# Delta rule and MLP: chunks of 32 tokens with all batches in a step, and the small inverses on VectorE

## The chip, the cores and the metric

The kernel runs on one NeuronCore of a Trainium2 chip. The metric is the device time of one execution, in microseconds (us). The core has a matrix engine (TensorE, PE in the profile; PEld is its loading of the stationary operand), three engines for elementwise work (VectorE = DVE, ScalarE = ACT, GpSimd = POOL) and SyncE (SP), which here only issues DMAs. TensorE writes to PSUM, 8 banks of 2 KB on each of 128 partitions; all else lies in SBUF.

## The reference

An attention block by the delta rule feeds an MLP. There are 4 batches, 8 heads, 768 tokens and a head dimension of 48; the MLP has 3072 tokens, 384 features and 2048 hidden units. All is float32.

```python
k_n = k / (np.linalg.norm(k, axis=-1, keepdims=True) + 1e-06)
for t in range(S):
    y[:, :, t] = einsum('bhd,bhde->bhe', q[:, :, t], state)
    v_old = einsum('bhde,bhd->bhe', state, k_n[:, :, t])
    state = state + beta_t * einsum('bhd,bhe->bhde', k_n[:, :, t], v_t - v_old)
x = y.transpose(0, 2, 1, 3).reshape(B * S, H * D)
h = x @ w_in
out = (h * clip(h + 3, 0, 6) / 6) @ w_out
```

## The kernel before

The tokens of a batch are cut into 6 chunks of C = 128; a step is one chunk of one batch with all 8 heads, so there are 24 steps, ordered so that batches 0 and 1 take turns and then batches 2 and 3. In a chunk that starts with the state S0, with L[i, j] = beta_j k_i.k_j for j < i, the kernel solves (I + L) Z = V - K S0, gives Y = Q S0 + strict_lower(Q K^T diag(beta)) Z, and adds (diag(beta) K)^T Z to the state.

For each step, `prep` (L260 to L273) normalises the keys and multiplies them by beta on GpSimd. `inverse` (L300 to L389) transposes k, q and beta k on TensorE, forms the scores in PSUM (L322, on 64 rows of the array per head), masks them, and inverts the four 32 x 32 diagonal blocks of I + L by doubling the size of inverted blocks: four levels, each with two sets of 8 matmuls (L362 and L370) of 128 x 128 stationary and 32 moving columns, between which GpSimd and VectorE spread a compact matrix into a full one (`to_full`, L283). `MX` (L385) couples the blocks. `chain` (L395 to L477) is the serial part: R = V - K S0 (L416), three rounds of U (L406), Z (L406), Y (L442, L447), the state's update (L457, L467), and the transposes of Y into `xT` (L474). `mlp_block` (L480 to L513) takes 256 tokens: 16 hidden slices of 3 matmuls (L486), each followed by a ScalarE and a VectorE instruction (L491, L495), then 2 x 16 matmuls into the output (L503).

The loop at the end takes one piece of `chain(i)`, one of `inverse(i + 1)` and one of the MLP in turn. The tile framework treats the order in which the program emits instructions as a priority; the order of each engine's queue is fixed when the program is built, and on a queue an instruction waits for the semaphores of what it needs. The weights arrive as float64 bits; `load_rows` (L167 to L199) makes float32 of them in seven VectorE instructions a piece, eight pieces a step. All loads of q, k, v and the stores of the output are issued on SP's queue, those of the weights on GpSimd's.

Of the kernel before, what the change touches and what calls it, by code (L numbers as in the profile page):

```python
# [8 lines left out]
FP32 = mybir.dt.float32  # L9
# [8 lines left out]
def kernel(  # L18
# [23 lines left out]
    C, G, DP = 128, 32, 64  # L42
    NG = C // G
    NLEV = 5
    assert 2**NLEV == G and S % C == 0 and D <= DP and H % 4 == 0 and B % 2 == 0
    NCH = S // C
    NP = H // 2
    BH = B * H
    NKT = DM // 128
    NFC = FF // 128  # L50
    assert NKT * 128 == DM == H * D and NFC * 128 == FF and BH <= 128
    CB = 2
    TB = CB * C
    assert NCH % CB == 0
# [7 lines left out]
    psT = ctx.enter_context(tc.tile_pool(name="psT", bufs=1, space=PSUM))  # L62
    psA = ctx.enter_context(tc.tile_pool(name="psA", bufs=1, space=PSUM))
    psL = ctx.enter_context(tc.tile_pool(name="psL", bufs=2, space=PSUM))
    psC = ctx.enter_context(tc.tile_pool(name="psC", bufs=1, space=PSUM))
    psM = ctx.enter_context(tc.tile_pool(name="psM", bufs=2, space=PSUM))

    steps = [(g * 2 + i, c) for g in range(B // 2) for c in range(NCH) for i in range(2)]
    N = len(steps)
    kfs, vfs, invs, Fs = {}, {}, {}, {}  # L70

    def tokens(ap, i):
        b, c = steps[i]
        return ap[b, :, c * C : (c + 1) * C, :].rearrange("h t d -> t h d")

# [1 line left out]
    NKB, NBKB = 2, 3  # L77
    kbufs = [persist.tile([C, NP, 2, DP], FP32, name=f"kb{i}") for i in range(NKB)]
    qbufs = [persist.tile([C, NP, 2, DP], FP32, name=f"qb{i}") for i in range(NKB)]
    bkbufs = [persist.tile([C, NP, 2, DP], FP32, name=f"bkb{i}") for i in range(NBKB)]  # L80

    def heads(t):
        return t[:].rearrange("p a e w -> p (a e) w")[:, :, 0:D]

    def load_k(i):
        if i < N:
            kfs[i] = stage.tile([C, H, D], FP32, name="kf")
            nc.sync.dma_start(out=kfs[i][:], in_=tokens(k, i))

    def load_v(i):  # L90
        if i < N:
            vfs[i] = stage.tile([C, H, D], FP32, name="vf")
            nc.sync.dma_start(out=vfs[i][:], in_=tokens(v, i))

    def load_q(i):
        if i < N:
            nc.sync.dma_start(out=heads(qbufs[i % NKB]), in_=tokens(q, i))

    load_k(0)
    load_k(1)  # L100
    beta_fm = persist.tile([BH, S], FP32, name="beta_fm")
    nc.scalar.dma_start(out=beta_fm[:], in_=beta.rearrange("b h s -> (b h) s"))

    for t in kbufs + qbufs + bkbufs:
        nc.vector.memset(t[:, :, :, D:DP], 0.0)
    load_q(0)
    load_q(1)
    load_v(0)
    load_v(1)
    load_k(2)  # L110
    load_k(3)

# [4 lines left out]
    def select(view, pattern, base, mult, op=ALU.is_ge):  # L117
        nc.gpsimd.affine_select(
            out=view, in_=view, pattern=pattern, compare_op=op, fill=0.0, base=base,
            channel_multiplier=mult,  # L120
        )

    masks = []
    for lev in range(NLEV):
        # The lower left block of each 2s x 2s diagonal block, transposed.
        s = 2**lev
        m = const.tile([C, C], FP32, name=f"mask{lev}")
        mv = m[:].rearrange("p (b e s) -> p b e s", e=2, s=s)
        nc.gpsimd.memset(m[:], 0.0)
        nc.gpsimd.memset(mv[:, :, 1, :], 1.0)  # L130
        nb = C // (2 * s)
        select(m[:], [[-2 * s, nb], [0, 2 * s]], 0, 1)
        select(m[:], [[2 * s, nb], [0, 2 * s]], s - 1, -1)
        masks.append(m)
    mrest = const.tile([C, C], FP32, name="mrest")
    nc.gpsimd.memset(mrest[:], 1.0)
    select(mrest[:], [[G, NG], [0, G]], -1, -1)
    mdiag = const.tile([C, NG, G], FP32, name="mdiag")
    nc.gpsimd.memset(mdiag[:], 1.0)
    select(mdiag[:], [[-G, NG], [0, G]], 0, 1)  # L140
    select(mdiag[:], [[G, NG], [0, G]], G - 1, -1)
    mstrict = const.tile([C, C], FP32, name="mstrict")
    nc.gpsimd.memset(mstrict[:], 1.0)
    select(mstrict[:], [[1, C]], 0, -1, ALU.is_gt)

# [21 lines left out]
    def load_rows(dst, src, w):  # L167
        """Float32 rows of a weight matrix. It may come as the bits of float64: sign, 11 bits of
        exponent, 52 of mantissa, low word first."""
        if w.dtype == FP32:  # L170
            nc.gpsimd.dma_start(out=dst, in_=src)
            return
# [405 lines left out]
```

## Time and profile before

| | us |
|---|---|
| three runs | 1664.49, 1666.99, 1675.18 |
| median of the runs | 1666.99 |
| the profiled execution: span from its first to its last instruction | 1664.9 |
| TensorE busy in it | 1510.3 |
| VectorE, GpSimd, ScalarE busy | 692.7, 404.9, 250.0 |

The page gives no time beside the span for the profiled execution; what lies around the span is therefore read from the runs, whose median is 2.1 us above it. In the rows that are shown further down, "L362 PE MATMUL ps<-Xc,Af 128*128 128x32 f32 x1536 | 231.9, 312 | 19.0 <-DVE" reads: line 362, engine and operation, the output's name and the operands' names, the rows and columns of the stationary operand, the output's partitions and elements with their type, the count, busy time in us, mean duration of one in ns, and the engine's idle time in front of them in us with what ended it. Busy time counts stretches once where instructions overlap, which on TensorE they do; so busy time divided by the count is less than the mean duration. The granted clock is the share of full speed at which TensorE was allowed to run.

### The profile page before, as it was taken

To read this page: it belongs to the slowest core of one execution; us is meant where nothing else is said; L and a number is where in the kernel's file an instruction comes from. 1 tells how busy PE (TensorE), PEld (TensorE's weight loads), DVE (VectorE), ACT (ScalarE), POOL (GpSimd) and SP (SyncE) were. 2 spreads that over 40 slices of the span, in tenths; PEclk is the share of its full clock that TensorE was granted. 3 is DMA by queue.
4 is the path that set the end of the run, shared out by engine and by line. 5 is a ranking of instruction groups with operands and counts; after the bars stand their busy time and mean duration, and the time that the engine had idled before them with its cause. 6 is when DMAs were issued, how large, how long until landed. Compare 5 with 4: busy or idle time off the path is not lost.

```text
span 1664.9 us, 20256 instructions
## 1 busy us (share of the span) xinstructions
PE 1510.3 (91%) x8526; PEld 1298.6 (78%) x8526; DVE 692.7 (42%) x1428; ACT 250.0 (15%) x601; POOL 404.9 (24%) x253
## 2 busy tenths in 40 slices
PE   4687879899998999997999998999998999998999
PEld 3676868788877886886887877986886887887876
DVE  7665666724424243343243333243343343342211
ACT  2000010201201121211121201021111111211111
POOL 4222322222222122223122231132222222222100
PEclk9999986889996599998799997599998899997799
DMA  5111121101000001000001000000000000000000
GB/s 107 48 56 44 48 57 43 29 1 25 15 6 19 5 11 24 15 6 19 6 10 24 15 6 19 5 11 19 11 6 19 6 6 15 1 6 6 0 10 10
DMA packets 81483, 32.86 MB, mean 20 GB/s; under 512 B 75728, under 2 KB 78800, under 8 KB 81392
## 3 DMA queue, kind: packets, MB, share of 16 engines
q1 hardware_dynamic: 78336, 18.88, 5.4%
q0 software_dynamic: 3008, 12.58, 2.4%
q8 instruction: 67, 1.10, 0.3%
q14 instruction: 24, 0.20, 0.0%
q10 hardware_dynamic: 48, 0.10, 0.0%
HBM read 26.84 MB, written 4.72 MB: 19 GB/s over the span
## 4 chain that ended last, share of the span: by engine, by line
PE 82%; DVE 8%; issue 4%; POOL 4%; ACT 1%; POOLq 0%; DMA 0%; SPq 0%; ACTq 0%; DVEq 0%
PE ph L486 16%; PE ps L362 13%; PE po L503 13%; PE ps L370 12%; PE pc L406 10%; PE px L385 4%; PE pa L322 4%; PE pc L447 3%; POOL Xf L283 3%; PE pt L307 2%; PE pc L457 2%; PE pc L442 1%; PE pc L416 1%; DVE Pf L283 1%; DVE Wc L374 1%
## 5 line engine op out<-in xcount | busy, mean ns | idle before, releaser
L486 PE MATMUL ph<-xT,w_in 128*128 128x256 f32 x1152 | 326.0, 426 | 0.0
L283 POOL TENSOR_TENSOR Af<-Ac,mask 128x1024 f32<-128x1024 f32 x96 | 226.9, 2377 | 233.1 <-ACT Ac L334 163.0
L503 PE MATMUL po<-w_out,g 128*128 128x384 f32 x768 | 273.3, 498 | 0.0
L362 PEld LDWEIGHTS ps<-Xc,Af 128*128 128x128 f32 x1536 | 233.8, 237 | 33.4 <-issue 23.5
L486 PEld LDWEIGHTS ph<-xT,w_in 128*128 128x128 f32 x1152 | 226.6, 211 | 32.4 <-issue 3.3
L362 PE MATMUL ps<-Xc,Af 128*128 128x32 f32 x1536 | 231.9, 312 | 19.0 <-DVE Xc L295 19.0
L370 PEld LDWEIGHTS ps<-Wc,Pf 128*128 128x128 f32 x1536 | 226.4, 229 | 25.9 <-DVE Pf L283 16.3
L370 PE MATMUL ps<-Wc,Pf 128*128 128x32 f32 x1536 | 223.7, 305 | 12.5 <-DVE Pf L283 12.5
L283 DVE TENSOR_TENSOR Pf<-ps,mdiag 128x1024 f32<-128x1024 f32 x96 | 117.6, 1225 | 224.6 <-PE ps L362 224.6
L503 PEld LDWEIGHTS po<-w_out,g 128*128 128x128 f32 x768 | 140.8, 193 | 81.9 <-issue 8.0
L491 ACT ACTIVATE t<-ph,half 128x256 f32<-128x256 f32 x192 | 91.2, 475 | 483.9 <-PE ph L486 462.8
L283 POOL TENSOR_TENSOR Wf<-Wc,mdiag 128x1024 f32<-128x1024 f32 x24 | 57.3, 2388 | 384.9 <-DVE Wc L374 384.9
L374 DVE TENSOR_TENSOR Wc<-Wc,ps 128x256 f32<-128x256 f32 x96 | 40.5, 421 | 238.1 <-PE ps L370 238.1
L495 DVE SCALAR_TENSOR_TENSOR g<-t,ph 128x256 f32<-128x256 f32 x192 | 80.5, 419 | 137.8 <-ACT t L491 135.2
L385 PE MATMUL px<-Arest,Xf 128*128 128x128 f32 x384 | 65.2, 339 | 68.2 <-POOL Xf L283 68.2
L385 PEld LDWEIGHTS px<-Arest,Xf 128*128 128x128 f32 x384 | 60.0, 246 | 77.7 <-POOL Xf L283 77.6
L406 PEld LDWEIGHTS pc<-U,MX 128*128 128x128 f32 x768 | 101.1, 209 | 13.7 <-DVE U L430 3.0
L406 PE MATMUL pc<-U,MX 128*128 128x48 f32 x768 | 102.4, 291 | 0.3 <-DVE U L430 0.3
L406 PE MATMUL pc<-U,Wf 128*128 128x48 f32 x384 | 60.0, 321 | 27.6 <-DVE U L430 27.6
L406 PEld LDWEIGHTS pc<-U,Wf 128*128 128x128 f32 x384 | 58.5, 238 | 33.6 <-DVE U L430 31.2
L322 PE MATMUL pa<-KQ,BK 64*128 64x256 f32 x384 | 76.8, 451 | 2.5 <-DVE Bm L339 1.8
L271 POOL TENSOR_TENSOR bkb<-kb,beta_tok 128x384 f32<-128x384 f32 x24 | 21.9, 914 | 229.6 <-PE pc L457 229.4
(88 smaller groups left out, 1363.7 us busy)
## 6 DMA issues: line engine op xcount, KB each, us to landing
d<-in_moe_w_in_dram POOLq DMA_DIRECT2D x12, 512.0 KB, 4.2
d<-in_moe_w_out_dram POOLq DMA_DIRECT2D x16, 384.0 KB, 3.3
kf<-in_k_dram SPq DMA_DIRECT2D x24, 192.0 KB, 3.1
qb<-in_q_dram SPq DMA_DIRECT2D x24, 192.0 KB, 2.9
vf<-in_v_dram SPq DMA_DIRECT2D x24, 192.0 KB, 2.6
out_dram<-o SPq DMA_DIRECT2D x24, 192.0 KB, 1.9
beta_fm<-in_beta_dram ACTq DMA_DIRECT2D x1, 96.0 KB, 3.2
```

The costliest lines, as they stand in the source:

```text
L283: eng.tensor_tensor(out=dst[:].rearrange("p h (a r) -> p h a r", r=G), in0=src.unsqueeze(2).to_broadcast([C, H, NG, G]), in1=m.unsqueeze(1 ...
L322: nc.tensor.matmul(pa[:, e, pp].rearrange("p j w -> p (j w)"), lhsT=BK[r, 2 * g + pp, :], rhs=KQ[r, 2 * g + pp].rearrange("p j w -> p (j w)"),
L362: nc.tensor.matmul(ps[:, h, :], lhsT=Af[:, h, :], rhs=Xc[:, h, :], start=True, stop=True)
L370: nc.tensor.matmul(ps[:, h, :], lhsT=Pf[:, h, :], rhs=Wc[:, h, :], start=True, stop=True)
L374: nc.vector.tensor_tensor(out=Wn[:], in0=Wc[:], in1=ps[:], op=ALU.subtract)
L385: nc.tensor.matmul(ps[:, h, :], lhsT=Xf[:, h, :], rhs=Arest[:, h, :], start=True, stop=True)
L406: nc.tensor.matmul(ph[:, D * h : D * h + D], lhsT=m[:, h, :], rhs=z[:, D * h : D * h + D], start=True, stop=True,)
L447: nc.tensor.matmul(py[:, D * h : D * h + D], lhsT=F["Bm"][:, h, :], rhs=Z[:, D * h : D * h + D], start=(c == 0), stop=True, skip_group_che ...
L486: nc.tensor.matmul(ph[:], lhsT=w_in[:, s, f * 128 : (f + 1) * 128], rhs=xT[:, s, :], start=(s == 0), stop=(s == NKT - 1),)
L491: nc.scalar.activation(out=t1[:], in_=ph[:], func=ACTF.Relu, bias=half[:, 0:1], scale=1.0 / 6.0)
L495: nc.vector.scalar_tensor_tensor(out=g[:], in0=t1[:], scalar=1.0, in1=ph[:], op0=ALU.min, op1=ALU.mult)
L503: nc.tensor.matmul(po[:], lhsT=gs[f][:, t * 128 : (t + 1) * 128], rhs=w_out[:, f, :], start=(f == 0), stop=(f == NFC - 1),)
```

## The change

Chunks become 32 tokens long, and a step holds one chunk of all four batches: partition 32 b + c is token c of batch b, and there are again 24 steps. With 32 x 32 systems there are no blocks to couple. Four steps form a group of 4 x 8 x 4 = 128 systems:

- `prep(t)` makes KQ (8 transposes in place of 12) and the scores in 64-row by 32-column tiles of the array, with the factor beta and the mask put on by one VectorE instruction (LB). The strictly triangular L goes to a DRAM scratch, 32 numbers at a time.
- `inverse(g)` loads the group's 128 systems with one system on each partition, inverts them all by substitution on VectorE (30 columns, two instructions each), stores the result to DRAM and loads it back into LB, step by step.
- `chain(t)` is R, one product with the inverse, Y and the update, with no rounds of U. The products by head are 32 x 32 tiles on the array's diagonal, the products with the state 128 x 32 tiles, the update 32 x 128 tiles; the state of all batches lies in one tile.
- The MLP's blocks are as before (256 tokens, now 2 steps of all batches). The weights' pieces of w_in are 256 wide instead of 512, all weights are issued after the first two steps, on SP's queue.
- The final loop runs a block's two chains with the next group's preps between their pieces, then the previous MLP block in one piece, then, after every second block, the next group's inverse.

```diff
+    C, DP = 32, 64
+    P = B * C
+    N = S // C
+    GS = 4
+    scratch = ctx.enter_context(tc.tile_pool(name="scratch", bufs=1, space=bass.MemoryType.DRAM))
+    psP = ctx.enter_context(tc.tile_pool(name="psP", bufs=1, space=PSUM))
+    psC = ctx.enter_context(tc.tile_pool(name="psC", bufs=4, space=PSUM))
+    psM = ctx.enter_context(tc.tile_pool(name="psM", bufs=2, space=PSUM))
...
+    def prep(t):
...
+        KQ = work.tile([128, NP, 2, P], FP32, name="KQ", bufs=7)
+        pt = psP.tile([128, 2, NP, P], FP32, name="pt", tag="pp")
+        for j, src in enumerate((kb, qb)):
+            for p in range(NP):
+                nc.tensor.transpose(
+                    pt[:, j, p, :], src[:, 2 * p : 2 * p + 2].rearrange("p e w -> p (e w)"), ident[:]
+                )
+            nc.scalar.activation(out=KQ[:, :, j, :], in_=pt[:, j], func=ACTF.Copy)
+        load_q(t + NQB)
+        yield
+        sc = psP.tile([P, 2, 512], FP32, name="sc", tag="pp")
+        scv = sc[:, :, 0 : NP * 2 * C].rearrange("p e (a j w) -> p e a j w", a=NP, j=2)
+        for p in range(NP):
+            for b in range(B):
+                for e in range(2):
+                    r = slice(DP * e, DP * e + DP)
+                    nc.tensor.matmul(
+                        scv[rows(b), e, p],
+                        lhsT=KQ[r, p, 0, rows(b)], rhs=KQ[r, p, :, rows(b)],
+                        start=True, stop=True,
+                    )
+        LB = work.tile([P, 2, NP, 2, C], FP32, name="LB", bufs=7)
+        nc.vector.tensor_tensor(
+            out=LB[:].rearrange("p e a j w -> p e (a j w)"), in0=sc[:, :, 0 : NP * 2 * C],
+            in1=mb[:].rearrange("p e a j w -> p e (a j w)"), op=ALU.mult,
+        )
...
+        nc.sync.dma_start(
+            out=l_dram[g][i].rearrange("h p c -> p h c"),
+            in_=LB[:].rearrange("p e a j w -> p (e a) j w")[:, :, 0, :],
+        )
...
+    def inverse(g):
+        A = work.tile([128, C, C], FP32, name="A", bufs=1)
+        nc.sync.dma_start(
+            out=A[:].rearrange("p c i -> p (c i)"),
+            in_=l_dram[g][:].rearrange("t h (b c) i -> (t h b) (c i)", b=B),
+        )
+        for j in range(1, C - 1):
+            n = C - 1 - j
+            pr = work.tile([128, C * C // 4 - C // 2], FP32, name="pr", bufs=1)
+            pv = pr[:, 0 : j * n].rearrange("p (c i) -> p c i", c=j)
+            nc.vector.tensor_tensor(
+                out=pv, in0=A[:, j, j + 1 :].unsqueeze(1).to_broadcast([128, j, n]),
+                in1=A[:, 0:j, j].unsqueeze(2).to_broadcast([128, j, n]), op=ALU.mult,
+            )
+            nc.vector.tensor_tensor(
+                out=A[:, 0:j, j + 1 :], in0=A[:, 0:j, j + 1 :], in1=pv, op=ALU.subtract
+            )
...
+        nc.sync.dma_start(
+            out=x_dram[g][:].rearrange("t h (b c) i -> (t h b) (c i)", b=B),
+            in_=A[:].rearrange("p c i -> p (c i)"),
+        )
+        for i in range(GS):
+            LBv = LBs[g * GS + i][:].rearrange("p e a j w -> p (e a) j w")
+            nc.sync.dma_start(out=LBv[:, :, 0, :], in_=x_dram[g][i].rearrange("h p c -> p h c"))
...
+        def of_heads(ph, m, z, start):
+            for h in range(H):
+                for b in range(B):
+                    nc.tensor.matmul(
+                        ph[rows(b), D * h : D * h + D], lhsT=m(h)[rows(b)],
+                        rhs=z[rows(b), D * h : D * h + D],
+                        start=start, stop=True, skip_group_check=True,
+                        tile_position=(C * b, C * b),
+                    )
+        def of_state(ph, j, start):
+            for p in range(NP):
+                for b in range(B):
+                    nc.tensor.matmul(
+                        ph[rows(b), 2 * D * p : 2 * D * (p + 1)],
+                        lhsT=KQ[:, p, j, rows(b)], rhs=state[:, b, p, :],
+                        start=start(p), stop=True, skip_group_check=True,
+                        tile_position=(0, C * b),
+                    )
...
+        of_heads(ph, lambda h: LBv[:, he(h), 0, :], R, True)
...
+            of_state(py, 1, lambda p: p == 0)
+        of_heads(py, lambda h: LBv[:, he(h), 1, :], Z, t == 0)
...
+                        lhsT=bkb[rows(b), 2 * p : 2 * p + 2].rearrange("p e w -> p (e w)"),
+                        rhs=Z[rows(b), 2 * D * p : 2 * D * (p + 1)],
+                        start=True, stop=True, tile_position=(C * b, 0),
...
+    run(prep_group(0))
+    run(inverse(0))
+    for blk in range(N // CB):
+        for c in range(CB):
+            t = blk * CB + c
+            g, i = divmod(t, GS)
+            if i == 0:
+                load_k(g + 2)
+                preps = prep_group(g + 1)
+            load_v(t + 2)
+            ch = chain(t)
+            while next(ch, "end") != "end":
+                if i < 2:
+                    next(preps, None)
+            if i < 2:
+                next(preps, None)
+        if blk == 0:
+            for w in weights:
+                load_rows(*w)
+        if i == 1:
+            run(preps)
+        if blk > 0:
+            run(mlp_block(blk - 1))
+        if i == 1 and (g + 1) * GS < N:
+            run(inverse(g + 1))
+    run(mlp_block(N // CB - 1))
```

More of the change, by code (lines that the diff above doesn't have):

```diff
@@ L79 @@
[L79 to L93, printed above, removed]
@@ L95, in load_q, with rows @@
-    def load_q(i):
-        if i < N:
-            nc.sync.dma_start(out=heads(qbufs[i % NKB]), in_=tokens(q, i))
-    load_k(0)
[L100 to L111, printed above, removed]
+    def rows(b):
+        return slice(C * b, C * b + C)
@@ L114 @@
+    for b in range(B):
+        nc.scalar.dma_start(out=beta_hm[C * b : C * b + H, :], in_=beta[b])
+    for t in qbufs + kbufs + bkbufs:
+        nc.vector.memset(t[:, :, D:DP], 0.0)
+    for t in range(4):
+        load_q(t)
     ident = const.tile([128, 128], FP32, name="ident")
     make_identity(nc, ident[:])
[L117 to L136, printed above, removed]
```

416 lines of the change are left out of this document (141 added, 275 removed).

## The prediction

> **What bounds the kernel now.** I read the page's busy shares first, then the chain that ended last, then two stretches of the span (busy time and count of each engine, granted clock, DMA), then where the MLP's line begins.
>
> ```profile
> span 1664.9 us, 20256 instructions
> PE 1510.3 (91%) x8526; PEld 1298.6 (78%) x8526; DVE 692.7 (42%) x1428; ACT 250.0 (15%) x601; POOL 404.9 (24%) x253
> PE 82%; DVE 8%; issue 4%; POOL 4%; ACT 1%; POOLq 0%; DMA 0%; SPq 0%; ACTq 0%; DVEq 0%
> 0.00:276.00 276.00, 204.23 (x895) 185.43 (x896) 176.79 (x389) 27.08 (x68) 84.61 (x92) 0.93 0.23 59
> 276.00:1570.00 1294.00, 1217.48 (x7229) 1048.00 (x7229) 501.51 (x1007) 206.64 (x500) 315.68 (x160) 0.89 0.05 12
> L486 PE MATMUL ph<-xT,w_in x1152: 379/379/775, 276.1 to 1640.1; 128*128 128x256 f32 x192
> ```
>
> TensorE holds 82% of the last chain, and between 276 us (the MLP's first matmul) and 1570 us it is busy 1217.48 of 1294 us, 94%. So the end is set by the sum of TensorE's work. The next question is what that work consists of.
>
> ```profile
> L486 PE MATMUL ph<-xT,w_in 128*128 128x256 f32 x1152 | 326.0, 426 | 0.0
> L503 PE MATMUL po<-w_out,g 128*128 128x384 f32 x768 | 273.3, 498 | 0.0
> L362 PE MATMUL ps<-Xc,Af 128*128 128x32 f32 x1536 | 231.9, 312 | 19.0 <-DVE Xc L295 19.0
> L370 PE MATMUL ps<-Wc,Pf 128*128 128x32 f32 x1536 | 223.7, 305 | 12.5 <-DVE Pf L283 12.5
> L406 PE MATMUL pc<-U,MX 128*128 128x48 f32 x768 | 102.4, 291 | 0.3 <-DVE U L430 0.3
> L322 PE MATMUL pa<-KQ,BK 64*128 64x256 f32 x384 | 76.8, 451 | 2.5 <-DVE Bm L339 1.8 <-DVE nt L244 0.7
> 1619.80 20.72 PE ph L486 x96
> 1640.51 20.66 PE po L503 x64
> ```
>
> A float32 matmul appears twice (the reference needs 576 for L486, the row counts 1152); I call one entry with its weight load a pair. The MLP (L486, L503) takes 599 us of busy time. It stays. The last block, alone and at full clock, shows its price: 20.72/96 = 0.216 us a pair at 256 columns, 20.66/64 = 0.323 at 384. The other 6606 pairs take 1510 - 599 = 911 us, 0.138 each, though most stream only 32 or 48 columns. The next view says why.
>
> ```profile
> 908.98 1.94 PE L362 MATMUL ps<-Xc,Af 128*128 128x32 f32 x16
> 920.22 1.97 PE L486 MATMUL ph<-xT,w_in 128*128 128x256 f32 x8
> 899.15 1.13 PE L322 MATMUL pa<-KQ,BK 64*128 64x256 f32 x8
> 46.78 3.64 PE ps L370 x16
> L362 PE MATMUL ps<-Xc,Af x1536: 192/276/402, 31.7 to 1568.3; 128*128 128x32 f32 x192
> L307 PE MATMUL pt<-ident,kb 128*128 128x128 f32 x96 | 30.8, 321 | 3.7 <-POOL kb L267 2.1 <-DVE BK L311 1.6
> ```
>
> Sixteen pairs of 32 columns take 1.94 us: less the last one's own 0.276 us, 15 steps of 0.111 us. A pair eight times wider costs only twice that, so a narrow pair is bounded by something else, of which the 128-column weight load is the nearest candidate. Where the clock is low the same sixteen take 3.64 us. And eight pairs of 256 columns that use 64 rows take 1.13 us against 1.97 us for eight that use 128: **two tiles of the array run side by side**.
>
> **The change, part by part.** The order of instructions is fixed when the program is built, but not as emitted: on TensorE, transposes L307 of the second step stand at 35 us between L362 and L370 of the first.
>
> ```profile
> 31.71 3.59 PE L362 MATMUL ps<-Xc,Af 128*128 128x32 f32 x16 [6.59 <-DVE Xc L295]
> 35.11 0.45 PE L307 MATMUL pt<-ident,kb 128*128 128x128 f32 x1
> 36.69 1.70 PE L370 MATMUL ps<-Wc,Pf 128*128 128x32 f32 x7 [0.69 <-DVE Pf L283]
> ```
>
> So I assume that the new loops, which emit chain, MLP block and inverse one behind the other, will be mixed too: MLP matmuls fill the waits inside a chain. That is an assumption about the changed kernel; its price if false is the fourth rival.
>
> *Removed from TensorE:* L362, L370, L385 (MX), L406 (three rounds U and Z), a third of the transposes L307. *Added, a step of 32 tokens x 4 batches (24 steps):* scores 32 matmuls = 64 pairs of 64 columns; the two triangular products 2 x 32 = 128 pairs of 48; the two state products 2 x 16 = 64 pairs of 96; the update 16 = 32 pairs with 128-column weights: **288 pairs, 6912 in all, more than the 6606 now**. The change pays only if a pair gets cheaper. Bounds from rows:
> - no gain in loading or side by side: 0.111 us, 32.0 us a step;
> - each pair its own stream only (0.216/256 = 0.84 ns a column; update 0.111 for its full load), one after another: 128 x 0.041 + 64 x 0.054 + 64 x 0.081 + 32 x 0.111 = 17.4 us;
> - two side by side, as the 64-row tiles show: 8.7 us; four: 4.4 us.
>
> I take 0.050 us a pair, 14.4 us a step: between one and two wide, nearer to one, because no row shows narrow pairs following faster than 0.109 us in a long run. With it, a step has 11 transposes (30.8/96 = 0.32 busy when alone, 0.11 in a row): 1.2 us. Every change of tile shape costs a gap:
>
> ```profile
> PEld pa L322 <- issue: 8.4, 32, 0.8
> PEld po L503 <- issue: 8.0, 25, 0.3
> ```
>
> 8.4/32 = 0.26 into the 64-row shape, 8.0/25 = 0.32 out of it. I count nine changes a step (into and out of scores, state products, first product, then product and update): 9 x 0.25 = 2.2 us. The MLP costs (20.72 + 20.66)/2 = 20.7 us a step at full clock and 599/24 = 25.0 by today's busy time (granted clock 0.89); I take 22.7. **Sum 14.4 + 1.2 + 2.2 + 22.7 = 40.5 us a step, 972 us.**
>
> *VectorE.* Rows:
>
> ```profile
> L244 DVE TENSOR_TENSOR nt<-nt,seed 128x16 f32<-128x16 f32 x12 | 2.1, 176 | 0.3
> L374 DVE TENSOR_TENSOR Wc<-Wc,ps 128x256 f32<-128x256 f32 x96 | 40.5, 421 | 238.1 <-PE ps L370 238.1
> L467 DVE TENSOR_TENSOR state<-state,pc 64x192 f32<-64x192 f32 x40 | 14.1, 352 | 11.4 <-PE pc L457 11.1
> L495 DVE SCALAR_TENSOR_TENSOR g<-t,ph 128x256 f32<-128x256 f32 x192 | 80.5, 419 | 137.8 <-ACT t L491 135.2
> L283 DVE TENSOR_TENSOR Pf<-ps,mdiag 128x1024 f32<-128x1024 f32 x96 | 117.6, 1225 | 224.6 <-PE ps L362 224.6
> L421 DVE TENSOR_TENSOR R<-vf,pc 128x384 f32<-128x384 f32 x20 | 11.1, 554 | 104.0 <-PE pc L416 104.0
> L196 DVE TENSOR_TENSOR e<-e,f 128x384 f32<-128x384 f32 (+1 forms) x28 | 22.5, 803 | 0.1
> ```
>
> From 16 to 256 elements (the latter read from PSUM) the duration grows 245 ns in 240, about 1.02 ns an element on 0.16 us. The substitution has j from 1 to 30, two instructions each, of j(31 - j) elements: 60 x 0.16 + 2 x 4960 x 0.00102 = 19.7 us, with 0.04 us between dependent ones **22 us a group, 133 us for six**. State updates are 8 x 23 x 0.352 = 65; MLP g stays 80.5; the weights' conversion, seven instructions a piece of which L196 is the costliest (22.5), stays below 158; LB, R, seam and squares' sums at about 0.55 to 0.7 each are 24 x 2.4 = 57, the norms' small ones 6 x 16 x 0.2 = 19. Sum at most 513 us against 692.7 today: Pf (117.6) and its kin go. VectorE does not become the bound. Its bursts (2.8 us of state updates) delay an MLP g at times; with two PSUM banks that stalls TensorE about as long as a block of L486 fills, 1.3 us; that is inside the idle share below. POOL loses all Af, Wf, Xf and keeps some 3 us a step.
>
> *DRAM trip, the added waits.* Rows:
>
> ```profile
> kf<-in_k_dram SPq DMA_DIRECT2D x24, 192.0 KB, 3.1
> 0.81 1.07 SPq L88 DMA_DIRECT2D kf<-in_k_dram  x2
> ```
>
> A load of 1024 pieces of 192 B lands in 3.1 us; LB out and X back are 1024 pieces of 128 B. One turn is 3.1 (LB out) + 3.1 (A in) + 22 + 3.1 (out) + 3.1 and three more issues of about 0.5 us = **36 us**. It starts when the group's four preps are done, which the 7 buffers of LB allow once the first step of the group before is through, and is due about three steps later, some 120 us. So I cost it at nothing; MLP and chains of the group before cover it. Behind the waiting A load on SP stand loads of v, k, q and the out stores, issued one or more steps ahead; behind the first product on TensorE, MLP matmuls. About 480 DMAs of 0.54 us occupy SP for 260 us, not the bound.
>
> *Start and end.*
>
> ```profile
> L310 ACT ACTIVATE KQ<-pt 128x256 f32<-128x256 f32 x96 | 36.8, 383 | 178.0 <-PE pt L307 178.0
> L388 ACT ACTIVATE MX<-px 128x1024 f32<-128x1024 f32 x24 | 24.6, 1025 | 254.1 <-PE px L385 254.1
> ```
>
> By these two a KQ copy of 512 elements takes about 0.6 us. A prep is 0.9 (transposes) + 1.2 (two copies) + 3.2 (64 pairs) + 0.7 (LB) and some waits, 6.5 us, and one PSUM slot keeps the four apart: 26. A chain is 3.2 (state products) + 0.55 (R) + 3.2 + 0.5 (Z) + 3.2 + 1.6 (update) + 2.8 (state) = 15 us. With 16 us for k and norms, the trip of 36 us, longer since weight conversion mixes with it on VectorE, and two bare chains the MLP begins near 130 us, not 276. Of these TensorE works about 70, so 60 us idle; 10 us for the end.
>
> *Idle share.* Today 6% in the middle; the new chain waits more often for other engines, so I take 10%: 972/0.9 = 1080. **1080 + 70 = 1150 us**, against the profiled execution's span of 1664.9; the runs' median is 2.1 us above that span.
>
> What decides is whether a small pair can follow the last one that fast. The Trainium skill, page TensorE: Matmul & The Clock Gate, section "Wait — 56ns, not 53.3ns?", says that the sequencer may need about 62 ns for each matmul when it decodes in software. By it the pairs would cost 288 x 0.062 = 17.9 us a step and the sum 1245 us, as an estimate; no row here shows such narrow pairs, and the 0.109 us of the transposes leaves room for either.
>
> **The rivals.**
> 1. *Four tiles side by side:* 4.4 us instead of 14.4, a step 30.5, 732/0.9 + 70 = 880 us. For it: the 64-row tiles. Against it: nobody shows the queue delivering a pair every 15 ns.
> 2. *Issue-bound:* a pair still takes 0.111 us, whatever its tile: 32.0 + 26.1 = 58.1 us a step, 1394/0.9 + 70 = 1619 us. For it: no narrow run below 0.109 in any row.
> 3. *Slower:* the bursts of small tiles run at the low clock for part of the time, and a pair costs what narrow ones cost on average now, 0.138 to 0.151 (231.9/1536): 0.14 gives 40.3 + 26.1 = 66.4, 1594/0.9 + 70 = **1840 us**. It decides from 0.117 us a pair on: (1667 - 70) x 0.9/24 = 59.9, less 26.1, by 288. For it: 3.64 us at 46.78 us; more pairs than before. Against it: the two-tile row.
> 4. *The inverse is not covered:* TensorE waits for the trip in each of five turns, 36 us to 60 us where VectorE mixes other work in: 240 us, 1390 us. For it: one A buffer, SP in order. Against it: 7 LB buffers.
>
> **How the numbers follow.** Forecast 0.50; rivals 0.10, 0.12, 0.10, 0.18 in this order. The range leaves out rivals 1 and 3, 0.20: from 900 (above four tiles; two wide gives 34.8 a step, 998) to 1620 (issue-bound). One per cent is about what a measurement can tell here. Faster by over that: all but rival 3 and a little of rival 2, 0.88; within it 0.02; slower 0.10.
>
> **What will show it.** Right: groups of 64 entries with 32-wide tiles in about 3 us; MLP rows within the chains' waits; TensorE at 85% or more after 130 us; the substitution at 22 us a group with no TensorE wait behind the X load. Wrong: pairs at 0.11 or more; the granted clock near 0.5 in the bursts; TensorE idle before the first product of every fourth step; MLP blocks standing as one piece after the chains, which would mean that my mixing doesn't happen and each chain's 15 us is bare.

## The result, and the profile after

The changed kernel takes **895.02 us** (median of 4 runs, 893.03 to 900.8) against 1665.74 us (median of 4, 1658.0 to 1675.18) of the kernel before on the same chip: a ratio of 0.5385, 95% interval 0.5357 to 0.5413. The forecast was 1150 us. The direction was right; the time lies 5 us below the low end of the range, and next to the first rival's 880 us. Medians and ratios leave out runs in a slower state (over 1.5% above the fastest run of the same kernel); of experiment 1 that leaves two runs (1105.56 and 1093.01 us), and its profile is of a slower one (1110.67 us).

The page of the changed kernel: span, busy times, the chain that ended last.

```profile
span 891.2 us, 20964 instructions
PE 744.6 (84%) x9000; PEld 522.2 (59%) x9000; DVE 424.2 (48%) x1231; ACT 167.2 (19%) x337; POOL 73.3 (8%) x118
PE 69%; DVE 20%; issue 4%; DMA 3%; ACT 2%; SPq 1%; POOL 0%; DVEq 0%; POOLq 0%
```

TensorE's entries are 9000 for 8526, yet its busy time has halved, 744.6 for 1510.3 us. VectorE now holds 20% of the chain, for 8%. The groups, with shapes kept apart, say what a small pair (one entry with its weight load) costs:

```profile
L399 PE MATMUL ph<-xT,w_in 128*128 128x256 f32 x1152 | 273.4, 389 | 10.4 <-DVE w_in L165 7.3 <-DVE g L408 2.7
L416 PE MATMUL po<-w_out,g 128*128 128x384 f32 x768 | 262.0, 500 | 17.6 <-DVE w_out L165 17.6
L333 PE MATMUL pc<-state,KQ 128*32 128x96 f32 x1472 | 57.6, 261 | 29.1 <-DVE state L377 27.0 <-issue 1.7
L366 PE MATMUL su<-Z,bkb 32*128 32x96 f32 x736 | 48.4, 295 | 3.6 <-issue 1.6 <-ACT y L361 0.9 <-DVE state L377 0.8
L255 PE MATMUL sc<-KQ 64*32 64x64 f32 x1536 | 25.5, 256 | 6.2 <-ACT KQ L246 6.2
L323 PE MATMUL pc<-Z,LB 32*32 32x48 f32 x1536 | 25.0, 206 | 4.0 <-issue 3.3 <-ACT Z L353 0.6
L323 PE MATMUL pc<-R,LB 32*32 32x48 f32 x1472 | 22.3, 205 | 1.9 <-DVE R L346 1.1 <-issue 0.8
L243 PE MATMUL pt<-ident,kb 128*128 128x128 f32 x96 | 21.1, 350 | 32.5 <-POOL kb L222 26.3 <-DVE LB L261 5.3 <-DVE pr L286 0.9
L243 PE MATMUL pt<-ident,qb 128*128 128x128 f32 x96 | 19.6, 332 | 6.8 <-ACT KQ L246 6.2
L385 PE MATMUL yt<-ident,y 128*128 128x128 f32 x72 | 13.9, 306 | 4.6 <-DVE state L377 3.7
```

With the first step's 64 pairs (1.5 us, the same line on vf) the five small groups have 6816 pairs and 180.3 us of busy time, 0.0265 us a pair and 7.5 us a step. That counts, beside the pairs' spacing, what each burst's last pair takes by itself. A chain in the steady part, TensorE alone (start, duration, group, count):

```profile
437.36 0.87 PE L333 MATMUL pc<-state,KQ 128*32 128x96 f32 x32
438.16 1.13 PE L399 MATMUL ph<-xT,w_in 128*128 128x256 f32 x4
439.22 0.88 PE L323 MATMUL pc<-R,LB 32*32 32x48 f32 x64
440.03 0.87 PE L333 MATMUL pc<-state,KQ 128*32 128x96 f32 x32
440.83 0.95 PE L323 MATMUL pc<-Z,LB 32*32 32x48 f32 x64
441.70 1.80 PE L366 MATMUL su<-Z,bkb 32*128 32x96 f32 x32
443.43 0.70 PE L399 MATMUL ph<-xT,w_in 128*128 128x256 f32 x2
```

Less the last pair's own 0.205 us, 63 steps of L323 take 0.675 us: **10.7 ns a pair**, on four tiles of the array in turn. MLP matmuls (L399) do stand in the chain's waits, two or four at a time, and no idle gap is left at a change of tile shape. (By these rows, less the last pair's own 0.20 or 0.25 us, the next burst's first pair starts 0.12 to 0.18 us after the last one's. That is an estimate, and it counts as busy time.) Three stretches of the span (length, then busy time and count of PE, PEld, DVE, ACT and POOL, the granted clock, DMA share, GB/s):

```profile
0.00:100.00 100.00, 31.29 (x720) 22.84 (x723) 44.47 (x147) 17.86 (x31) 28.66 (x59) 1.00 0.42 73
100.00:300.00 200.00, 137.10 (x2423) 91.24 (x2417) 180.90 (x546) 27.97 (x55) 22.80 (x29) 0.83 0.49 112
300.00:850.00 550.00, 539.70 (x5729) 383.26 (x5728) 193.34 (x525) 114.25 (x236) 21.87 (x31) 1.00 0.14 28
```

The first 300 us again, cut at the first MLP matmul (124.3 us):

```profile
0.00:124.30 124.30, 50.98 (x1278) 37.94 (x1278) 57.76 (x180) 22.22 (x39) 35.46 (x67) 1.00 0.43 77
124.30:300.00 175.70, 117.41 (x1858) 76.15 (x1859) 167.61 (x514) 23.62 (x47) 16.00 (x20) 0.81 0.50 114
```

From 300 us on TensorE is busy 539.70 of 550 us, 98%. Nearly all that is lost lies before: 68.7 us in the first hundred, 62.9 in the next two, where VectorE is the full engine with 180.90 of 200 us. Cut at the first MLP matmul it is 73.3 us ahead of it and 58.3 behind. In the stretch behind it the granted clock is 0.81, so TensorE is slower there as well as idle. The longest waits of TensorE (total, times, longest):

```profile
PE pc L333 <- DVE state L377: 27.0, 7, 23.4
PE pt L243 <- POOL kb L222: 26.3, 2, 16.8
PE pc L323 <- DMA LB<-x_dram: 25.2, 1, 25.2
PE po L416 <- DVE w_out L165: 17.6, 12, 3.3
```

Each stands for one thing of the start: the first group's DRAM trip with its substitution (25.2 us once, and never again), the normalised keys of the first steps from GpSimd (26.3 us), a single wait of 23.4 us for a state update on VectorE, and the weights' conversion (L165).

### The profile page after: what moved, and what is told of

Read it like the earlier page. It is cut to its first block, busy times and chain, and to the rows that moved or that the text cites. A ratio compares the mean times of both kernels' runs of the same rounds, so it can differ in the third digit from the quotient of the medians.

```text
span 891.2 us, 20964 instructions
## 1 busy us (share of the span) xinstructions
PE 744.6 (84%) x9000; PEld 522.2 (59%) x9000; DVE 424.2 (48%) x1231; ACT 167.2 (19%) x337; POOL 73.3 (8%) x118
## 3 DMA queue, kind: packets, MB, share of 16 engines
q1 hardware_dynamic: 140352, 44.07, 24.1%
## 4 chain that ended last, share of the span: by engine, by line
PE 69%; DVE 20%; issue 4%; DMA 3%; ACT 2%; SPq 1%; POOL 0%; DVEq 0%; POOLq 0%
PE po L416 26%; PE ph L399 26%; PE pc L333 4%; PE su L366 4%; PE pc L323 4%; DVE state L377 3%; DVE A L290 3%; PE pt L243 3%; DVE pr L286 3%; PE sc L255 2%; DVE e L162 2%; DVE e L159 1%; DVE f L151 1%; DMA A<-l_dram 1%; ACT KQ L246 1%
## 5 line engine op out<-in xcount | busy, mean ns | idle before, releaser
L399 PE MATMUL ph<-xT,w_in 128*128 128x256 f32 x1152 | 273.4, 389 | 10.4 <-DVE w_in L165 7.3
L399 PEld LDWEIGHTS ph<-xT,w_in 128*128 128x128 f32 x1152 | 205.0, 191 | 58.0 <-DVE w_in L165 9.5
L416 PEld LDWEIGHTS po<-w_out,g 128*128 128x128 f32 x768 | 146.7, 193 | 123.2 <-DVE w_out L165 25.2
L377 DVE TENSOR_TENSOR state<-state,su 48x192 f32<-48x192 f32 x184 | 64.8, 352 | 97.8 <-PE su L366 92.9
L333 PE MATMUL pc<-state,KQ 128*32 128x96 f32 x1472 | 57.6, 261 | 29.1 <-DVE state L377 27.0
L333 PEld LDWEIGHTS pc<-state,KQ 128*32 128x32 f32 x1472 | 37.6, 114 | 52.0 <-DVE state L377 32.1
L261 DVE TENSOR_TENSOR LB<-sc,mb 128x512 f32<-128x512 f32 x24 | 16.6, 692 | 97.0 <-PE sc L255 87.7
L290 DVE TENSOR_TENSOR A<-A,pr 128x30 f32<-128x30 f32 (+9 forms) x180 | 59.7, 332 | 3.2
L286 DVE TENSOR_TENSOR pr<-A 128x30 f32<-128x30 f32 (+9 forms) x180 | 59.1, 328 | 4.5 <-DMA A<-l_dram 1.1
L246 ACT ACTIVATE KQ<-pt 128x512 f32<-128x512 f32 x48 | 28.7, 597 | 137.4 <-PE pt L243 137.1
L366 PE MATMUL su<-Z,bkb 32*128 32x96 f32 x736 | 48.4, 295 | 3.6 <-issue 1.6
L229 POOL TENSOR_TENSOR mb<-beta_tok,mask 128x256 f32<-128x256 f32 x48 | 30.1, 649 | 221.3 <-DVE LB L261 177.0
L243 PE MATMUL pt<-ident,kb 128*128 128x128 f32 x96 | 21.1, 350 | 32.5 <-POOL kb L222 26.3
L366 PEld LDWEIGHTS su<-Z,bkb 32*128 32x128 f32 x736 | 39.5, 191 | 11.9 <-issue 5.2
```

What stands on the lines that cost most here:

```text
L243: nc.tensor.transpose(pt[:, j, p, :], src[:, 2 * p : 2 * p + 2].rearrange("p e w -> p (e w)"), ident[:])
L246: nc.scalar.activation(out=KQ[:, :, j, :], in_=pt[:, j], func=ACTF.Copy)
L286: nc.vector.tensor_tensor(out=pv, in0=A[:, j, j + 1 :].unsqueeze(1).to_broadcast([128, j, n]), in1=A[:, 0:j, j].unsqueeze(2).to_broadcast( ...
L290: nc.vector.tensor_tensor(out=A[:, 0:j, j + 1 :], in0=A[:, 0:j, j + 1 :], in1=pv, op=ALU.subtract)
L333: nc.tensor.matmul(ph[rows(b), 2 * D * p : 2 * D * (p + 1)], lhsT=KQ[:, p, j, rows(b)], rhs=state[:, b, p, :], start=start(p), stop=True, ...
L366: nc.tensor.matmul(su[b][:, 2 * D * p : 2 * D * (p + 1)], lhsT=bkb[rows(b), 2 * p : 2 * p + 2].rearrange("p e w -> p (e w)"), rhs=Z[rows(b ...
```

## The experiments

Two questions. Is it tiles side by side that make a pair cheap, or only the narrower weight load? And what is the start made of? Medians are given with the ratio to the kernel before and its interval. The changed kernel was not run again beside the experiments, so two versions count as different only where these intervals don't overlap. TensorE's busy and idle time come from the first lines of each page.

**1. The same pairs, successive ones on one tile.**

```diff
-            for h in range(H):
-                for b in range(B):
+            for bs in [[0], [1], [2], [3]]:
+              for h in range(H):
+                for b in bs:
```

(likewise over the state products and the update; the scores take one half of the rows after the other)

> The loops over the batches become the outer ones in the scores, the products by head, the products with the state and the update, so that successive pairs fall on the same tile of the array; count, shapes and results stay. Theory side-by-side: the small pairs are cheap because their neighbours sit on other tiles and run at the same time; one after another they cost their own stream or load (0.041, 0.054, 0.081, 0.111 us), 17.4 us a step instead of the 4.8 that the steps in the trace give (128 x 0.0107 + 64 x 0.0096 + 64 x 0.0196 + 32 x 0.049), so up to 12.6 x 24 = 302 us more: 1120 to 1200 us. Rival narrow-load: 32 columns of weights load fast, and that alone explains it; then the order changes nothing: 895 us, within 1%.

1099.29 us, 0.6626 (0.6387 to 0.6864): 204 us slower than the changed kernel with the same pairs and loads. TensorE in a burst of scores and in one chain, and four microseconds of that burst:

```profile
475.96 4.09 PE L255 MATMUL sc<-KQ 64*32 64x64 f32 x64
...
524.47 1.93 PE L335 MATMUL pc<-state,KQ 128*32 128x96 f32 x32
...
527.39 2.48 PE L324 MATMUL pc<-R,LB 32*32 32x48 f32 x64
...
534.07 2.95 PE L369 MATMUL su<-Z,bkb 32*128 32x96 f32 x32
```

```profile
476.00:480.00 4.00, 4.00 (x66) 3.83 (x65) 0.92 (x3) 0.00 (x0) 0.83 (x1) 0.50 0.00 0
```

36 ns from one pair to the next in place of 10.7 for the products by head, at a granted clock of 1.00 (524 to 536 us). Its small groups sum to 418.1 us, 17.4 us a step. That is the figure which the prediction worked out for pairs one after another, but by luck: it holds bursts at half the granted clock, such as the scores above with 4.09 us, which take 2.40 at 1.00 (462.84 us). Part of the 204 us is therefore this clock (0.897 in the mean, for 0.960 in the changed kernel's profile); why it falls inside these bursts stays open. The first eight bursts of scores take 4.09 us too, before 93 us, where the profile grants 1.00, so its clock does not tell all.

**2. Two tiles in turn.** As above with `[[0, 1], [2, 3]]`.

> As the one with batches outermost, but batches go in twos: successive pairs alternate between two tiles. Theory side-by-side: 8.7 us a step instead of 4.8, up to 94 us more: 960 to 990 us. Rival narrow-load: 895 us, within 1%.

937.07 us, 0.5647 (0.5583 to 0.5712), 42 us above the changed kernel.

```profile
520.52 1.22 PE L335 MATMUL pc<-state,KQ 128*32 128x96 f32 x32
521.67 1.42 PE L324 MATMUL pc<-Z,LB 32*32 32x48 f32 x64
523.02 1.79 PE L369 MATMUL su<-Z,bkb 32*128 32x96 f32 x32
```

19 ns from pair to pair for the products by head. One, two, four tiles: 36, 19, 10.7 ns. So **the order in which pairs are issued** takes a pair from 36 to 10.7 ns: neighbours in the queue must lie on different tiles. The smaller tile alone gives the step before that: 36 ns where 32 columns with a 128x128 load took 111 in the kernel before. No run parts its narrow load from its fewer rows. The update, whose weights have 128 columns, gains nothing beyond two tiles: 1.79 us here, 1.80 in the changed kernel.

**3. Two of the seven conversion instructions of a weight piece** (the low words and the flush of small numbers are left out).

```diff
-            out=f[:], in0=hi, scalar=0xC0000000, in1=f[:],
+            out=dst.bitcast(U32), in0=hi, scalar=0xC0000000, in1=f[:],
...
-        e = stage.tile([128, n], U32, name="e", bufs=1)
... (and the five instructions behind it)
```

> The weights' conversion keeps two of its seven VectorE instructions: the low words and the flush of subnormal numbers are left out, the loads stay. Theory start: between 115 and 297 us the MLP waits for weights that VectorE converts, and the state updates wait behind them; 89 us of VectorE work less there gives 60 to 90 us: 805 to 835 us. Rival: the start is set by the keys' preparation and the DRAM trip; less than 20 us: 875 to 895 us.

842.45 us, 0.5078 (0.5023 to 0.5134): 53 us less, a little short of the theory's range and far from the rival's. Its 100 to 300 us, and its waits for the state update:

```profile
100.00:300.00 200.00, 177.68 (x2333) 124.67 (x2329) 128.87 (x373) 40.32 (x83) 16.72 (x21) 0.97 0.46 111
```

```profile
PE pc L320 <- DVE state L364: 5.3, 4, 2.3
```

TensorE is busy 40.6 us more there; the last weight is ready at 218 us instead of 298, and the wait of 23.4 us is gone. Over the whole span (839.8 for 891.2 us) TensorE is idle 36.8 us less, and its busy time is 14.6 us less too, with a granted clock of 0.97 for 0.83 in this stretch.

**4. No substitution** (the loop over 30 columns left out; the inverse is then I + L with a new diagonal, stored and loaded as before).

```diff
-        for j in range(1, C - 1):
... (the whole loop)
```

> The 30 columns of the substitution are left out, so that what comes back from DRAM is L itself with a new diagonal; the trip, its DMAs and the order stay. Theory hidden: only the first group's 24 us of VectorE stands on the path, and in the second group's place VectorE, busy with the weights, gains some 10 to 20: 25 to 45 us less, 850 to 870 us. Rival exposed: every group's 22 us counts: 133 us less, 762 us.

878.36 us, 0.5299 (0.5219 to 0.5378): 17 us less by the medians, short of the 25 to 45 expected; the interval just overlaps the changed kernel's, so the size is not sure. The same two views:

```profile
0.00:100.00 100.00, 51.08 (x1188) 38.15 (x1189) 34.26 (x107) 19.72 (x35) 31.12 (x62) 0.95 0.53 95
100.00:300.00 200.00, 152.80 (x2359) 102.20 (x2356) 163.62 (x423) 30.39 (x59) 24.63 (x32) 0.80 0.42 99
```

```profile
PE yt L372 <- DVE state L364: 6.5, 11, 1.7
```

The first trip's gap goes from 25.2 to 1.3 us, and the 23.4 us wait goes here too: TensorE is idle 35.5 us less (111.1 for 146.6). But its busy time is 17.5 us more (762.1 for 744.6), with a granted clock of 0.80 for 0.83 between 100 and 300 us and 0.95 for 1.00 before; no run shows what lowers it. The conversion still ends at 294 us, yet the waits for weights don't grow (19.7 us for 24.9). In the steady part TensorE is idle 10.3 us with the substitutions and without. So the later ones are covered, as forecast, though the busy time of all six is 118.8 us (rows of L286 and L290, 59.1 and 59.7).

**5. The weights' conversion emitted behind the first inverse,** not behind the first two steps.

```diff
     run(inverse(0))
+    for w in weights:
+        load_rows(*w)
...
-        if blk == 0:
-            for w in weights:
-                load_rows(*w)
```

> The weights are emitted behind the first group's inverse instead of behind the first two steps, so their conversion ranks ahead of the first chain and may fill VectorE's idle time from 20 us on. Theory start: conversion, which now runs from 115 to 297 us, begins up to 80 us earlier, at the cost of a later first inverse; what leaving five of seven instructions out gained (53 us) is in reach: 845 to 875 us. Rival: the first chain, pushed behind conversions, comes as much later: 890 to 910 us.

873.4 us, 0.5244 (0.5211 to 0.5278): **the fastest version that computes everything**, 2.6% below the changed kernel, and the two intervals don't touch. The conversion runs from 65 to 236 us. The price is that it mixes with the first substitution, which takes 31 us from first to last instruction instead of 24. TensorE's longest waits:

```profile
PE pc L323 <- DMA LB<-x_dram: 36.8, 1, 36.8
PE yt L385 <- DVE state L377: 31.2, 3, 27.8
```

Both are longer than in the changed kernel, and TensorE's idle time falls by only 5.2 us (141.4 for 146.6). The larger part of the gain is busy time, 16.6 us less (728.0 for 744.6), with a granted clock of 0.88 for 0.83 between 100 and 300 us. No run shows what sets that clock.

**6. Emitted ahead of the first inverse too.**

> The weights are emitted ahead of the first group's inverse too. Theory start: conversion begins by 45 us, but each substitution instruction now ranks behind it, so the first inverse takes longer by the conversions that get in between; gain and loss are of one size: 850 to 900 us. Rival: only the end of conversion counts; then it is the fastest of the orders: 830 to 850 us.

879.09 us, 0.528 (0.5243 to 0.5318). The conversion ends at 234 us, about as in 5, and the wait of 28 us near 162 us stands as before. The time lies in the theory's wide range, but not as the theory has it: the conversion does not begin by 45 us, it begins at 64.6, where version 5 begins it (64.7). The two intervals overlap; the place matters little once it is early.

**7. The MLP block emitted ahead of its two chains.**

```diff
     for blk in range(N // CB):
+        if blk > 0:
+            run(mlp_block(blk - 1))
         for c in range(CB):
```

> The MLP block is emitted ahead of the block's two chains instead of behind them, so it ranks higher, and chains get TensorE only where it waits. Theory mixing: the MLP's matmuls no longer fill the chains' waits; R 0.55, Z 0.5, state updates 2.8 and hand-overs, some 5 us a step, stand bare, though preps fill a part: 60 to 120 us more: 955 to 1015 us. Rival: chains of later steps or preps fill them just as well: 890 to 910 us.

928.9 us, 0.558 (0.5541 to 0.5618), 34 us slower, between the two forecasts. Its steady part:

```profile
300.00:850.00 550.00, 525.90 (x5274) 376.08 (x5273) 186.51 (x509) 110.01 (x227) 21.87 (x31) 0.97 0.14 27
```

The steady part is idle for 24.1 us, not 10.3: with less MLP work left over for a chain's waits, as I read it. Over the whole span TensorE is idle 22.5 us more and busy 12.1 more (granted clock 0.942 for 0.960). What this order takes away of the mixing is worth some 35 us, less than the 60 to 120 that bare waits would have cost; no run does without mixing altogether.

**8. Version 5 with the conversion's addition on GpSimd** (and a second buffer for e).

```diff
-        nc.vector.tensor_tensor(out=ef, in0=ef, in1=f[:].bitcast(FP32), op=ALU.add)
+        nc.gpsimd.tensor_tensor(out=ef, in0=ef, in1=f[:].bitcast(FP32), op=ALU.add)
```

> As with the weights behind the first inverse, and the addition among the seven conversion instructions goes to GpSimd, with a second buffer for it. Theory start: VectorE has 20 us less, GpSimd some 30 more beside 73: 5 to 20 us faster than with the addition on VectorE. Rival: hand-overs between the engines and the slower GpSimd make each piece longer: as fast or up to 20 us slower than that.

888.75 us, 0.5342 (0.5304 to 0.538): 15 us slower than version 5. The rival was right: VectorE is busy 409.8 us for 419.4, half of what was hoped, and it now waits for GpSimd's addition 24 times, 17.4 us in all. The longest wait for a state update shrinks from 27.8 to 9.5 us, which does not make up for it.

**9 and 10. Version 5 with the second inverse's substitution emitted in pieces between the links of the next two chains (9), and all five later ones (10).**

```diff
             while next(ch, "end") != "end":
                 if i < 2:
                     next(preps, None)
+                next(inv, None)
...
-            run(inverse(g + 1))
+            inv = inverse(g + 1)
```

> As the version with early weights, but the second inverse's substitution (the one that runs beside the weights' conversion) is emitted in six pieces between the links of the next two chains, not in one piece. Theory: in all versions in which a full substitution and the full conversion alternate on VectorE (the changed kernel 133.7 to 157.1 us, the early-weights version 162.4 to 190.1) TensorE waits 23 to 28 us once, because the state update stands behind that whole stretch in VectorE's own order; cut up, no wait of TensorE after 110 us is longer than 8 us and the time is 850 to 862 us, against 873.4. Rival: VectorE is simply full until the conversion ends (some 235 us), so the same wait comes back in smaller pieces: 868 to 880 us.

> As the one before, but all five later substitutions are emitted in pieces between the links of the two chains that follow, not beside an MLP block. Theory: beside an MLP block a substitution costs nothing, between the links of a chain five columns (about 3.7 us) stand ahead of a product R, a Z-dependent state update or LB; with some 7 pieces in each of the four turns that are not the first and half of it not covered by MLP matmuls, 4 x 7 x 1.8 = 50 us over the version that cuts only the first: 895 to 920 us. Rival: the order of emission hardly matters, since MLP matmuls fill the chains' waits anyway: within 8 us of that version.

879.07 us, 0.5264 (0.5231 to 0.5297), and 885.93 us, 0.5316 (0.5272 to 0.536). The wait stayed; the waits of version 9, and VectorE in order of time, show why:

```profile
PE yt L385 <- DVE state L377: 36.8, 4, 33.3
```

```profile
156.86 0.18 DVE L286 TENSOR_TENSOR pr<-A 128x30 f32<-128x30 f32 x1
...
193.52 0.21 DVE L290 TENSOR_TENSOR A<-A,pr 128x30 f32<-128x30 f32 x1
193.63 0.33 DVE L377 TENSOR_TENSOR state<-state,su 48x192 f32<-48x192 f32 x1
```

The program was cut, the queue was not: the substitution still stands in one stretch from 156.86 to 193.52 us, alternating with the conversion, and the state update directly behind it. In version 10, too, each substitution from the third on stands in one stretch of 23 to 26 us. So neither run tested its theory. What is shown is that the wait ends with that stretch, and, by experiments 3 and 4, that lightening either half of the mixture removes it.

**11. Each 32x32 product as two of half the columns.** Same columns, same tiles in turn, twice the pairs.

```diff
             for h in range(H):
+              for w0 in (0, D // 2):
                 for b in range(B):
+                    s0 = slice(D * h + w0, D * h + w0 + D // 2)
```

> As the changed kernel, but each 32x32 product by head is issued as two of half the columns (24 and 24 in place of 48): twice the pairs in L323's bursts (128 for 64), the same columns streamed, and the same tiles in turn. A pair of the 64 took 10.7 ns in the changed kernel, and one tile's next pair thus came 43 ns after its last. Theory A, each tile is bound by its own stream (0.84 ns a column, 40 ns for 48 columns; four at a time 10 ns): the half-wide pairs take 5 to 7 ns each (the 32-column load, 0.84 ns a column by the same rate, is 27 ns, four at a time 6.7), a burst of 128 lasts 0.85 to 1.1 us, and the time is within 10 us of the changed kernel. Theory B, TensorE can't start a float32 pair more often than about every 10 ns whatever its width: a burst of 128 lasts 1.5 us, 0.63 us more, and with 2 bursts in each of 24 steps the time is 895 + 30 = 925 us.

991.73 us, 0.5964 (0.5915 to 0.6012): 97 us slower, and by neither theory. TensorE in a chain:

```profile
461.86 1.13 PE L401 MATMUL ph<-xT,w_in 128*128 128x256 f32 x4
462.92 1.24 PE L325 MATMUL pc<-R,LB 32*32 32x24 f32 x125
464.93 0.24 PE L325 MATMUL pc<-R,LB 32*32 32x24 f32 x3 [0.77 <-issue]
465.10 0.87 PE L335 MATMUL pc<-state,KQ 128*32 128x96 f32 x32
465.89 0.97 PE L325 MATMUL pc<-Z,LB 32*32 32x24 f32 x93
468.93 0.73 PE L325 MATMUL pc<-Z,LB 32*32 32x24 f32 x35 [2.06 <-issue]
```

Within a burst the pair costs (1.24 - 0.190)/124 = 8.5 ns, between the theories' 5 to 7 and 12. But the burst now breaks off in its middle, waiting for nothing that the profile shows. The page's row of the instruction queue, of the changed kernel and of this one:

```profile
q8 instruction: 71, 1.16, 0.5%
```

```profile
q8 instruction: 95, 1.56, 0.7%
```

Twenty-four more loads of 16,384 bytes for 3072 more pairs, that is 6144 instructions: 64 bytes each, 256 instructions or 128 pairs a load. Between the two breaks stand 3 + 32 + 93 = 128 pairs, just one load; between two later ones (815.23 and 818.97 us) 122 of this product and 6 of the update. By the trace's transfer records loads landed at 463.70 and 467.69 us, and TensorE went on 1.23 and 1.24 us after each. So I read **the supply of instructions** as a bound of its own: bursts live on what was loaded ahead during the MLP block, and beyond that a load of 128 pairs comes every 3.6 to 4.0 us (these two start at 462.58 and 466.18 us), 28 to 31 ns a pair. This was read from the breaks; no run varied the loading itself. Nor is it the whole loss: TensorE is idle 37.9 us more than in the changed kernel and busy 55.9 us more, at a mean granted clock of 0.911 for 0.960. The changed kernel stays just inside the supply: its five small groups waited 7.4 us in all for "issue" (sum of their rows), here the larger of L325's groups alone 29.1:

```profile
L325 PE MATMUL pc<-Z,LB 32*32 32x24 f32 x3072 | 40.2, 195 | 29.7 <-issue 29.1 <-ACT Z L355 0.6
```

## Why the prediction was wrong in size and right in direction

**The step that failed is the term "0.050 us a pair, 14.4 us a step".** It was bounded by 17.4, 8.7 and 4.4 us for one, two and four tiles side by side, and taken near one "because no row shows narrow pairs following faster than 0.109 us". By busy time the runs gave 17.4 us a step on one tile (experiment 1), 10.0 on two (239.8 us in experiment 2) and 7.5 on four, of which the update, which stops at two tiles, is 2.0. The spacing of the pairs in the shortest full burst of each group, added up as the prediction did it, comes to 12.8, 7.3 and 4.9 us, an estimate; what is above it stands in the ends of bursts and in slower bursts. So the four-tile bound had the spacing nearly right and left out the ends of bursts; the 17.4 came true by luck. The choice between the bounds was wrong. The 64-row row (1.13 us for eight pairs against 1.97) did show tiles side by side; the absence of a faster row was an absence of narrower tiles, and was weighed as if it were evidence.

**The sum, term by term** (TensorE's busy time; predicted, then measured, us): small pairs 345.6 and 180.3; changes of tile shape 52.8 and no idle time that a row shows (by the estimate above, what they take stands in the small pairs' 180.3); MLP 544.8 and 535.4; transposes 28.8 and 54.6 (pt and yt; they stand in twos and threes between other work, not in a long row). The groups overlap by 25.7 us; 972 and 744.6 in all. Idle: 178 (108 in the middle, 70 at both ends) and 146.6 (in the middle 58.3 from 124.3 to 300 us and 10.3 to 850; at the ends 73.3 before the first MLP matmul and 4.7 behind 850 us). So -227.4 and -31.4 make up the difference between 1150 and the span of 891.2.

**The idle share, 10%, came out in size by luck and lay in the wrong place.** From the first MLP matmul to 850 us TensorE is idle for 68.6 of 725.7 us, 9.5%, but 58.3 of it lie before 300 us, and the steady part loses 2%. The assumption behind it, that MLP matmuls fill a chain's waits, is right in kind (the chain's rows above, experiment 7), and a chain is some 10 us long with them in it, not 15 without.

**The start was costed to the wrong point.** Up to the first MLP matmul the forecast was near: it came at 124.3 us, for 130, with 73.3 us idle, for 60. What that matmul was to find there, the weights, was not costed. "VectorE does not become the bound" is true of its sum (424.2 us for at most 513) and false where it counts: between 100 and 300 us it is 90% busy with conversion and substitutions mixed, and TensorE waits for w_in, w_out and once for a state update behind them. Experiment 3 shows it: a shorter conversion takes away 36.8 us of idle time. An earlier one (experiment 5) takes away 5.2; it gives 22 us in all, for the most part as busy time at a higher granted clock.

**The DRAM trip at nothing** held but for the first group (25.2 us, which the prediction had in its start). The substitution takes 19.8 us busy and 24 us long, for 22.

**The rivals.** Four tiles side by side (0.10) is what came. That its 880 us lie so near 895 is partly luck: it has 158 us for pairs and changes of shape together, for 180.3, and 26 us too little for transposes, while the overlap of 25.7 us, the MLP and the idle time (151 us for 146.6) cancel most of that. Its reason against, "nobody shows the queue delivering a pair every 15 ns", was the right question: a queue filled ahead delivers one every 10.7 ns, and one that is not breaks off (experiment 11). Issue-bound at 0.111 us and slower at 0.14 are excluded by 10.7 to 49 ns a pair. The slower rival's row (3.64 us at 46.78 us) stands where the profile grants a clock of 1.00 (40 to 52 us), so the prediction's "where the clock is low" is not shown by it; its sign, a granted clock near 0.5 in the bursts, came true in experiment 1 and not in the changed kernel, which has 1.00 from 300 to 850 us. The estimate at 17.9 us a step adds up to 1243 us by the prediction's own terms, not 1245, and was refuted with the others. The uncovered inverse would have shown a wait for x_dram in every turn; there is one.

## What to carry to other kernels

Small matmuls on small tiles of the array pay in full only if neighbours in the queue lie on different tiles; the loop order over the same products was worth 204 us here, and a bound worked out from "one, two, four side by side" deserves to be believed as a range with both ends open until a run has been made. An engine's sum over the whole span does not say whether it is the bound in one stretch: do the sum for the start by itself, with one-off work such as converting weights in it. When a version is faster, split the gain into idle and busy time: experiments 4 and 5 look alike by their medians and are not. When pairs become cheap, count instructions as well as time, since more, smaller ones (experiment 11) cost more than the same columns in fewer.

## What the runs showed of the hardware that was not expected

*Pairs of float32 on 32x32 tiles start 10.7 ns apart on four tiles, 19 on two, 36 on one.* The Trainium skill, page TensorE: Matmul & The Clock Gate, section "Wait — 56ns, not 53.3ns?", gives about 62 ns a matmul with software decode and about 25 ns as the least distance of two starts; these bursts on two and four tiles lie below both, and the measurement decides. The same page's section "Measured speedup vs the span model" gives some 4 ns for each further tile side by side, as an overhead of issue. The runs go the same way, at 10.7 ns, with a new weight load for each pair and each tile used again after four pairs.

*Instructions come in loads of 256, and small pairs can outrun them* (experiment 11). No estimate had this.

*GpSimd can be held off for a whole substitution.* In version 5 one product on GpSimd, 0.83 us elsewhere, lasts 28.89 us, though the profile's spans of GpSimd are rough. VectorE is meanwhile in the mixed stretch of substitution and conversion, most of whose instructions have two operands; one of them with a single operand, 0.35 us elsewhere, takes 0.98 across the moment at which GpSimd comes free. In experiments 1, 6, 7 and 11, too, such products last 24 to 32 us, each beside a substitution. The timeline, GpSimd's row and VectorE's:

```profile
157.73 28.89 POOL L235 TENSOR_TENSOR bkb<-kb,beta_tok 128x384 f32<-128x384 f32 x1 [8.31 <-PE su L366]
```

```profile
185.85 0.98 DVE L147 TENSOR_SCALAR f<-d 128x384 uint32<-128x384 uint32 x1
```

The Trainium skill, page SBUF — State Buffer, section "SBUF: two separate sides", describes the port pair that VectorE and GpSimd share as an exclusive lock, in which the loser waits entirely. These two rows agree with it in kind, though the page speaks of a single instruction and here GpSimd waits through a whole stretch of short ones. In experiment 8, where VectorE waits for GpSimd within the mixture, none of GpSimd's 40 additions lasts longer than 1.05 us, so that run's loss is no case of it. No run here took the lock away alone, and it remains an explanation of the rows.
